# One attention-decode and dense kernel: scores and softmax run two heads ahead of the values, dense and projection weights pass through the value buffers, deeper rings, and the last output-projection rows come last

## The chip, the cores and the metric

The kernel runs on one core of a Trainium2 chip. The metric is the device time in microseconds of one execution. Its engines work side by side, each through its own list of instructions in order: TensorE (PE in the profile; PEld is its weight load), VectorE (DVE), ScalarE (ACT), GpSimd (POOL) and SyncE (SP), which issues the loads. Semaphores tie the lists together.

## What is computed

Two tokens (batch 2, one position each) of width 448 pass through an attention block with a key and value cache and through a dense block with the mish activation; both results are added to the input. The window is the last 4096 of 32768 positions; there are 8 key/value heads of width 256, each shared by 2 query heads.

```python
xn = layernorm(x)                                   # x: 2 x 1 x 448
q = xn @ wq                                         # 16 heads x 256
scores = einsum("bhqd,bhkd->bhqk", q, k[last 4096]) * 256 ** -0.5
o = einsum("bhqk,bhkd->bhqd", softmax(scores), v[last 4096])
attn = o.reshape(2, 1, 4096) @ wo                   # wo: 4096 x 448
h = xn @ w1 + b1                                    # w1: 448 x 1792
dense = (h * tanh(softplus(h))) @ w2                # w2: 1792 x 448
out = x + attn + dense
```

## The kernel before

There are 16 pairs of a key/value head and a batch row, called heads here and numbered i = 0 to 15 (batch row 0, then 1, of each key/value head). Each has a key tile and a value tile of 2 MB (128 partitions, 32 positions each). A head is worked in two halves, so the main loop has 32 steps s; step s is half s % 2 of head s // 2. For one half:

- `turn(s)`: VectorE transposes half of the key tile in blocks (`kt`, L345);
- `scores(s)`: TensorE multiplies the transposed keys with a block-diagonal query `qdiag` (8 matmuls, L357); ScalarE takes the exponential into `p` and its row sums into `rs` (L367);
- `values(s)`: VectorE transposes `p` to `pT` (L380); TensorE multiplies it with half of the value tile (32 matmuls into `o`, L402). In the second half of a head TensorE also sums the denominators (`den`, L389), VectorE takes their reciprocal `rec` and writes the scaled head to `oT` (L415), and for every second head TensorE adds `oT` times the rows `wo` of this key/value head to the result `psA` (8 matmuls, L195, in the helper `add`).

`build_q` has GpSimd fill `qdiag` for a later head. `project` computes the queries from `wq`; `dense_in` and `dense_out` are the dense block, from weights `w1` and `w2` that `load_dense` brings.

All large loads are issued by SyncE in the order of the code: `load_k`, `load_v`, `load_wo`, `load_dense`. Tiles come from pools with a fixed number of buffers: keys 3, values 3, wo 3, with places of their own for `wq`, `w1` and `w2`. A load into a buffer waits until the tile that was there has been used: a key load for the transposition of the second half of the key three heads older (VectorE), a value load for the values three heads older (TensorE). Eight semaphores (DMAHW0 to DMAHW7 in the listings) are used in turn for landings, so a load also waits for the landing of the one eight loads before it. At the end of the code `issue_in_order` pins every engine's instructions to the order in which they are written, so the calls in the loop set each engine's order:

```python
        if s + 1 < NSTEP:
            turn(s + 1)
        if s < NSTEP:
            scores(s)
        if s >= 1:
            values(s - 1)
```

`values(s - 1)` thus stands on TensorE between `scores(s)` and `scores(s + 1)`. Dense loads are issued at step 3, `dense_in` follows step 9 and `dense_out` step 11. After the last step VectorE and ScalarE copy `psA` to `res`, and SyncE stores it.

Of the kernel before, what the change touches and what calls it, by code (L numbers as in the profile page):

```python
# [11 lines left out]
BF16 = mybir.dt.bfloat16  # L12
FP32 = mybir.dt.float32
# [21 lines left out]
def kernel(  # L35
# [13 lines left out]
    nc = tc.nc  # L49
    P = 128  # L50
    Q = 32
# [46 lines left out]


    wq_sb = weights.tile([P, NS, HW], BF16)  # L100
    wq_in = A_wq.rearrange("r (x n) -> (r x) n", x=NX).rearrange("(p s) n -> p s n", s=NS)
    SC = NS // 2 + 1
    nc.sync.dma_start(out=wq_sb[:, 0:SC, :], in_=wq_in[:, 0:SC, :])  # L103
    nc.sync.dma_start(out=wq_sb[:, SC:NS, :], in_=wq_in[:, SC:NS, :])  # L104

# [96 lines left out]
    wq_v = wq_sb[:, :, :].rearrange("p s (h m e) -> p s h e m", h=HH, e=NE)  # L202

    def project():
        qT_ps = ps_m.tile([P, HH, NE, NX * Bsz], FP32, tag="m", name="qT_ps")
        for hh in range(HH):
            for e in range(NE):
                for s in range(NS):
                    nc.tensor.matmul(  # L209
                        qT_ps[:, hh, e, :],  # L210
                        lhsT=wq_v[:, s, hh, e, :],
                        rhs=xs[:, s, :, :].rearrange("p x b -> p (x b)"),
                        start=(s == 0),
                        stop=(s == NS - 1),
                    )
# [28 lines left out]
    w1_sb = weights.tile([P, NS, HF], BF16)  # L244
    w2_sb = weights.tile([P, NX, NF, D], BF16)
    act_bf = consts.tile([P, NF, NX, Bsz], BF16)

    def load_dense():
        nc.sync.dma_start(
            out=w1_sb[:],  # L250
            in_=B_w1.rearrange("r (x n) -> (r x) n", x=NX).rearrange("(p s) n -> p s n", s=NS),
        )
        nc.sync.dma_start(
            out=w2_sb[:], in_=B_w2.rearrange("(x q c) d -> q x c d", x=NX, q=P)
        )

    def dense_in():
        w1_v = w1_sb[:].rearrange("p s (q c) -> p s c q", c=NF)
# [38 lines left out]
    def dense_out():  # L297
        for x in range(NX):
# [12 lines left out]
    LAST = (0, TH, TH + TH // 2, T)  # L311
    k_t, kt_t, v_t, p_t, wo_t = {}, {}, {}, {}, {}
# [10 lines left out]
    def load_v(i):  # L323
        kvh, b = heads[i]
        t = v_pool.tile([P, T, Dh], BF16, tag="v", name="v")
        vin = A_v_cache[b, kvh, s0:Sk, :].rearrange("(p t) d -> p t d", p=P)
        cuts = LAST if i == len(heads) - 1 else (0, T)
        for lo, hi in zip(cuts, cuts[1:]):
            nc.sync.dma_start(out=t[:, lo:hi, :], in_=vin[:, lo:hi, :])
        v_t[i] = t  # L330

    def load_wo(kvh):
        w = wo_pool.tile([P, rep, ND * D], BF16, tag="wo", name="wo")
        r0 = kvh * rep * Dh
        nc.sync.dma_start(
            out=w[:],
            in_=A_wo[r0 : r0 + rep * Dh, :].rearrange("(h p c) d -> p h (c d)", h=rep, p=P),
        )
        wo_t[kvh] = w
# [36 lines left out]
    def values(s):  # L376
        i, half = divmod(s, NH)
        kvh, b = heads[i]
        pT = p_pool.tile([P, TH * Q], BF16, tag="pT", name="pT")
        nc.vector.transpose(out=pT[:], in_=p_t.pop(s)[:])  # L380
        pTv = pT[:].rearrange("p (t c) -> p t c", t=TH)
        if half == 0:
            state["o", i] = ps_o.tile([P, ND, rep], FP32, tag="o", name="o")
        po = state["o", i]
        if half == NH - 1:
            rs = state.pop(("rs", i))
            den = ps_den.tile([P, rep], FP32, tag="den", name="den")
            for n in range(NH):
                nc.tensor.matmul(  # L389
                    den[:],  # L390
                    lhsT=rs[:, n : n + 1].to_broadcast([P, P]),
                    rhs=hsel[:],
                    start=(n == 0),
                    stop=(n == NH - 1),
                )
            rec = small.tile([P, rep], FP32, tag="rec", name="rec")
            nc.vector.reciprocal(out=rec[:], in_=den[:])  # L397
        v = v_t[i] if half < NH - 1 else v_t.pop(i)
        vv = v[:].rearrange("p t (m c) -> p t c m", c=ND)
        for t in range(TH):  # L400
            for c in range(ND):
                nc.tensor.matmul(  # L402
                    po[:, c, :],
                    lhsT=vv[:, half * TH + t, c, :],
                    rhs=pTv[:, t, 0:rep],
                    start=(half == 0 and t == 0 and c == 0),
                    stop=(half == NH - 1 and t == TH - 1),
                    skip_group_check=True,
                )
        if half != NH - 1:  # L410
            return
        if b == 0:
# [5 lines left out]
            in1=rec[:].unsqueeze(1).to_broadcast([P, ND, rep]),  # L418
            op=ALU.mult,
        )  # L420
        if b != Bsz - 1:
            return
        w = wo_t.pop(kvh)
        for n in range(NO):
            for h in range(rep):
# [8 lines left out]

    KA = 2
    for i in range(KA):
        load_k(i)
    load_wo(0)
# [4 lines left out]
    for s in range(NSTEP + 1):  # L443
        i, half = divmod(s, NH)
        if half == 0 and i < len(heads):
            if i + KA < len(heads):
                load_k(i + KA)
            load_v(i)
        if s == 3:
            load_dense()  # L450
        if s % (NH * Bsz) == 0 and s // (NH * Bsz) + 1 < Hkv:
            load_wo(s // (NH * Bsz) + 1)
        if s % NH == 0 and 0 < s < NSTEP - NH:
            build_q(s // NH + 1)
        if s + 1 < NSTEP:
            turn(s + 1)
        if s < NSTEP:
            scores(s)
        if s >= 1:
            values(s - 1)  # L460
        if s == 9:
            dense_in()
        if s == 11:
            dense_out()

# [35 lines left out]
```

## Time and profile before

| | |
|---|---|
| median of three runs | 202.58 us (202.35 to 204.18) |
| the profiled execution | 204.15 us, of which the span is 202.4 us |
| read from HBM | 77.67 MB |
| busy: TensorE, VectorE, ScalarE, GpSimd | 139.2, 102.9, 25.5, 24.9 us |
| granted TensorE clock, mean | 0.79 of full |

The span is the time from the first to the last instruction that the profile shows; the rest of the execution lies around it. Idle time of an engine costs nothing unless something on the way to the end waits for it, so the rows to look at are those of the resource that is always busy, and what happens when it isn't. "PEclk" and the column ahead of the DMA share in the windows view are the clock that TensorE was granted, as a part of full speed.

### The profile page before, as it was taken

How to read it: one execution, taken by the hardware profiler on the slowest of the kernel's cores; microseconds unless marked ns; L12 is line 12 of the kernel's file. 1: busy time of each engine (PE TensorE's matmuls, PEld its weight loads, DVE VectorE, ACT ScalarE, POOL GpSimd, SP SyncE). 2: the span in 40 equal slices, each digit the busy share in tenths (PEclk: the TensorE clock that was granted, in tenths of full speed). 3: DMA queues.
4: the chain of work that ended last, by engine and by line, in shares of the span. 5: the costliest groups of instructions: out<-in, count | busy, mean ns of one | idle time of the engine just before them, and what ended most of it. 6: DMA issues, size and time to landing. Idle time of an engine off the chain costs nothing.

```text
span 202.4 us, 3790 instructions
## 1 busy us (share of the span) xinstructions
PE 139.2 (69%) x1624; PEld 82.0 (41%) x1624; DVE 102.9 (51%) x137; ACT 25.5 (13%) x69; POOL 24.9 (12%) x138
## 2 busy tenths in 40 slices
PE   0262802969906849799999388856976596849993
PEld 0051202526303425565766145533534353426472
DVE  4607660191910564137748917473656455562921
ACT  5000200111010201101112102020112011201120
POOL 7006210020020100200202201120022002000000
PEclk9999995575555878855899969697979797975797
DMA  6999999999999999997999999999999999999200
GB/s 224 425 437 421 434 421 415 431 417 430 422 410 437 427 426 419 423 424 243 434 427 421 431 434 405 429 424 427 407 442 427 418 419 430 424 421 406 83 0 2
DMA packets 7802, 77.90 MB, mean 385 GB/s; under 512 B 741, under 2 KB 2793, under 8 KB 3306
## 3 DMA queue, kind: packets, MB, share of 16 engines
q1 hardware_dynamic: 7780, 77.66, 91.9%
q8 instruction: 12, 0.20, 0.4%
q14 instruction: 4, 0.03, 0.0%
q10 hardware_dynamic: 6, 0.01, 0.0%
HBM read 77.67 MB, written 0.00 MB: 384 GB/s over the span
## 4 chain that ended last, share of the span: by engine, by line
DMA 61%; PE 20%; DVE 15%; SPq 1%; issue 1%; ACT 1%
DMA v<-in_A_v_cache_dram 53%; DVE kt L345 12%; PE sc L357 10%; DMA k<-in_A_k_cache_dram 8%; PE o L402 6%; DVE pT L380 2%; PE hT_ps L263 2%; PE psA L195 1%; PE den L389 1%; SPq L318 1%; PE hT_ps L272 1%; DVE oT L415 0%; ACT p L367 0%; SPq L104 0%; SPq L103 0%
## 5 line engine op out<-in xcount | busy, mean ns | idle before, releaser
L357 PE MATMUL sc<-kt,qdiag 128*128 128x512 bf16 x256 | 86.3, 496 | 3.5 <-DVE kt L345 3.5
L345 DVE STREAM_TRANSPOSE kt<-k 128x2048 f32<-128x2048 f32 x32 | 73.1, 2287 | 2.3 <-DMA k<-in_A_k_cache_dram 2.3
L402 PE MATMUL o<-pT,v 128*128 128x2 bf16 x1024 | 30.8, 164 | 43.9 <-DMA v<-in_A_v_cache_dram 43.2
L402 PEld LDWEIGHTS <-v 128*128 128x128 bf16 x1024 | 30.8, 101 | 52.1 <-DMA v<-in_A_v_cache_dram 49.8
L357 PEld LDWEIGHTS <-qdiag 128*128 128x128 bf16 x256 | 27.4, 116 | 44.6 <-issue 29.4
L367 ACT ACTIVATE p<-sc 128x512 bf16<-128x512 f32 x32 | 19.1, 597 | 163.3 <-PE sc L357 163.3
L238 POOL COPY qdiag<-qrep 32x8 bf16<-32x8 bf16 x128 | 21.0, 187 | 143.2 <-PE sc L357 128.0
L397 DVE RECIPROCAL rec<-den 128x2 f32<-128x2 f32 x16 | 2.6, 166 | 62.5 <-PE den L389 62.5
L380 DVE STREAM_TRANSPOSE pT<-p 128x512 bf16<-128x512 bf16 x32 | 21.6, 674 | 3.0 <-ACT p L367 3.0
L389 PEld LDWEIGHTS den<-hsel,rs 128*128 128x128 f32 x64 | 12.9, 250 | 4.6 <-issue 3.3
L195 PE MATMUL psA<-wo,oT 128*2 128x224 bf16 x64 | 8.9, 291 | 2.0 <-DVE oT L415 2.0
L389 PE MATMUL den<-hsel,rs 128*128 128x2 f32 x64 | 10.2, 264 | 0.0
L415 DVE TENSOR_TENSOR oT<-o,rec 128x4 bf16<-128x4 f32 x16 | 2.6, 165 | 11.0 <-PE o L402 11.0
L209 PE MATMUL qT_ps<-xs,wq_sb 128*128 128x4 bf16 x112 | 3.3, 166 | 5.8 <-DMA wq_sb<-in_A_wq_dram 3.2
L195 PEld LDWEIGHTS <-oT 128*2 128x2 bf16 x64 | 5.2, 91 | 3.9 <-DVE oT L415 2.7
L367 ACT ACTIVATION_READ_ACCUMULATOR p<-sc 128x1 f32 x32 | 6.2, 194 | 0.0
L209 PEld LDWEIGHTS <-wq_sb 128*128 128x128 bf16 x112 | 3.1, 104 | 6.3 <-DMA wq_sb<-in_A_wq_dram 6.3
L163 PE MATMUL xnT_ps<-ident,xn_bf 2*128 2x2 bf16 x7 | 0.5, 166 | 5.0 <-DVE xn_bf L127 5.0
L282 DVE COPY h_sb<-hT_ps 128x28 f32<-128x28 f32 x1 | 0.2, 188 | 7.0 <-PE hT_ps L272 7.0
L263 PE MATMUL hT_ps<-xs,w_sb 128*128 128x4 bf16 x49 | 3.7, 195 | 0.0
L218 DVE CAST qT<-qT_ps 128x64 bf16<-128x64 f32 x1 | 0.2, 225 | 6.7 <-PE qT_ps L209 6.7
L263 PEld LDWEIGHTS <-w_sb 128*128 128x128 bf16 x49 | 3.2, 150 | 0.1
(40 smaller groups left out, 24.9 us busy)
## 6 DMA issues: line engine op xcount, KB each, us to landing
k<-in_A_k_cache_dram SPq DMA_DIRECT2D x16, 2048.0 KB, 16.1
v<-in_A_v_cache_dram SPq DMA_DIRECT2D x15, 2048.0 KB, 20.6
wo<-in_A_wo_dram SPq DMA_DIRECT2D x8, 448.0 KB, 21.1
w_sb<-in_B_w_dram SPq DMA_DIRECT2D x2, 1568.0 KB, 28.0
wq_sb<-in_A_wq_dram SPq DMA_DIRECT2D x1, 2048.0 KB, 7.6
wq_sb<-in_A_wq_dram SPq DMA_DIRECT2D x1, 1536.0 KB, 10.8
v<-in_A_v_cache_dram SPq DMA_DIRECT2D x1, 1024.0 KB, 13.0
v<-in_A_v_cache_dram SPq DMA_DIRECT2D x2, 512.0 KB, 14.3
```

Source lines behind the costliest of these rows:

```text
L195: nc.tensor.matmul(psA[n][:, :], lhsT=lhsT, rhs=rhs, skip_group_check=True, **flags)
L209: nc.tensor.matmul(qT_ps[:, hh, e, :], lhsT=wq_v[:, s, hh, e, :], rhs=xs[:, s, :, :].rearrange("p x b -> p (x b)"), start=(s == 0), stop=( ...
L238: nc.gpsimd.tensor_copy(out=tv[rows, :, e, j * Q : j * Q + rep], in_=qrep[rows, :, h0 : h0 + rep, e, x, b],)
L263: nc.tensor.matmul(hT_ps[:, c, :, :].rearrange("p x b -> p (x b)"), lhsT=w1_v[:, s, c, :], rhs=xs[:, s, :, :].rearrange("p x b -> p (x b)" ...
L345: nc.vector.transpose(out=kt[:].bitcast(FP32), in_=k[:, half * TH * Dh : (half + 1) * TH * Dh].bitcast(FP32),)
L357: nc.tensor.matmul(psc[:], lhsT=qdiag[i % NW][:, n * NE + e, :], rhs=ktv[:, n, e, :, :], start=(n == 0 and e == 0), stop=(n == NB - 1 and ...
L367: nc.scalar.activation(out=p_sb[:], in_=psc[:].rearrange("p t c -> p (t c)"), func=ACT.Exp, scale=scale, accum_out=state["rs", i][:, s % N ...
L380: nc.vector.transpose(out=pT[:], in_=p_t.pop(s)[:])
L389: nc.tensor.matmul(den[:], lhsT=rs[:, n : n + 1].to_broadcast([P, P]), rhs=hsel[:], start=(n == 0), stop=(n == NH - 1),)
L397: nc.vector.reciprocal(out=rec[:], in_=den[:])
L402: nc.tensor.matmul(po[:, c, :], lhsT=vv[:, half * TH + t, c, :], rhs=pTv[:, t, 0:rep], start=(half == 0 and t == 0 and c == 0), stop=(half ...
L415: nc.vector.tensor_tensor(out=oT[:, :, :, b], in0=po[:], in1=rec[:].unsqueeze(1).to_broadcast([P, ND, rep]), op=ALU.mult,)
```

## The change

Four things are changed.

1. `values` is split. `turn_p(s)` holds the transposition of `p`, the denominators and their reciprocal; `values(i)` holds all 64 value matmuls of a head and `oT`; `mix(kvh)` holds the wo matmuls. The loop goes over heads, and `values` of head i - 2 stands behind both sets of scores of head i. `pT` gets seven buffers, `p` three.
2. The pool `weights` is gone: the two parts of `wq`, then `w1` and `w2` are tiles of the value pool, which has five buffers; values 1 to 4 go into the buffers that they leave. The key pool has four buffers.
3. The dense loads are issued behind the first key, `dense_in` follows the scores of head 0, `dense_out` those of head 1.
4. `load_wo` of a key/value head stands behind its second value load in place of one key/value head ahead. The last value load is cut in halves (before: a half and two quarters), the last wo load in two pieces that are issued last of all.

```diff
-    weights = ctx.enter_context(tc.tile_pool(name="weights", bufs=1))
-    k_pool = ctx.enter_context(tc.tile_pool(name="kk", bufs=3))
-    v_pool = ctx.enter_context(tc.tile_pool(name="vv", bufs=3))
+    k_pool = ctx.enter_context(tc.tile_pool(name="kk", bufs=4))
+    v_pool = ctx.enter_context(tc.tile_pool(name="vv", bufs=5))
...
-    p_pool = ctx.enter_context(tc.tile_pool(name="pp", bufs=2))
+    p_pool = ctx.enter_context(tc.tile_pool(name="pp", bufs=3))
...
+    def v_tile(n):
+        t = v_pool.tile([P, T * Dh], BF16, tag="v", name="v")
+        return t[:, 0:n]
...
+    def turn_p(s):
+        pT = p_pool.tile([P, TH * Q], BF16, tag="pT", name="pT", bufs=7)
+        nc.vector.transpose(out=pT[:], in_=p_t.pop(s)[:])
+        pT_t[s] = pT
         i, half = divmod(s, NH)
+        if half != NH - 1:
+            return
+        rs = state.pop(("rs", i))
+        den = ps_den.tile([P, rep], FP32, tag="den", name="den")
...
+        nc.vector.reciprocal(out=state["rec", i][:], in_=den[:])
...
+    def mix(kvh):
+        oT = state["oT"]
         w = wo_t.pop(kvh)
-        for n in range(NO):
-            for h in range(rep):
+        for h in range(rep):
+            for n in range(NO):
                 for c in range(ND):
...
+    load_k(0)
+    load_dense()
+    load_k(1)
     project()
     build_q(0)
     build_q(1)
     turn(0)
...
+    for i in range(NK + KA):
+        if i + 2 < NK:
+            load_k(i + 2)
+        if i < NK:
+            load_v(i, parts=1 if i < NK - 1 else 2)
+            kvh, b = heads[i]
+            if b == Bsz - 1:
+                load_wo(kvh, parts=1 if i < NK - 1 else 2)
+            for half in range(NH):
+                s = i * NH + half
+                if s + 1 < NSTEP:
+                    turn(s + 1)
+                scores(s)
+                if s >= 1:
+                    turn_p(s - 1)
+            if i + 2 < NK:
+                build_q(i + 2)
+        if i == NK:
+            turn_p(NSTEP - 1)
+        if i == 0:
             dense_in()
-        if s == 11:
+        if i == 1:
             dense_out()
+        if i >= KA:
+            values(i - KA)
+            kvh, b = heads[i - KA]
+            if b == Bsz - 1:
+                mix(kvh)
```

Three places in the engines' order show the move. A row has the line, the operation, what it writes and from what, the tile's shape, and in brackets the engines or landing semaphores for which it waits.

SyncE at the start, before: from the two halves of `wq` on.

```order
L103 DMA wq_sb<-in_A_wq_dram 128x8192
L104 DMA wq_sb<-in_A_wq_dram 128x6144
L318 DMA k<-in_A_k_cache_dram 128x8192 x2
L335 DMA wo<-in_A_wo_dram 128x2x896
L318 DMA k<-in_A_k_cache_dram 128x8192
L329 DMA v<-in_A_v_cache_dram 128x8192 [waits DMAHW0_49]
L335 DMA wo<-in_A_wo_dram 128x2x896 [waits DMAHW1_49]
L318 DMA k<-in_A_k_cache_dram 128x8192 [waits DMAHW4_49,DMAHW2_49,DVE_49]
L329 DMA v<-in_A_v_cache_dram 128x8192 [waits DMAHW3_49]
L249 DMA w_sb<-in_B_w_dram 128x6272
L253 DMA w_sb<-in_B_w_dram 128x2x3136 [waits DMAHW5_49]
```

SyncE at the start, with the change; tiles named v that come from `wq` or `w` (the dense weights) are buffers of the value pool.

```order
L109 DMA v<-in_A_wq_dram 128x8192
L109 DMA v<-in_A_wq_dram 128x6144
L325 DMA k<-in_A_k_cache_dram 128x8192
L255 DMA v<-in_B_w_dram 128x6272
L260 DMA v<-in_B_w_dram 128x2x3136
L325 DMA k<-in_A_k_cache_dram 128x8192
L325 DMA k<-in_A_k_cache_dram 128x8192 [waits DMAHW0_49]
L336 DMA v<-in_A_v_cache_dram 128x8192 [waits DMAHW1_49]
L325 DMA k<-in_A_k_cache_dram 128x8192 [waits DMAHW2_49]
L336 DMA v<-in_A_v_cache_dram 128x8192 [waits DMAHW3_49,PE_49]
L345 DMA wo<-in_A_wo_dram 128x2x896 [waits DMAHW4_49]
L325 DMA k<-in_A_k_cache_dram 128x8192 [waits DMAHW5_49,DVE_49]
```

The dense weights moved from behind the second value to behind the first key, the wo load from behind the second key to behind the second value, and the fourth key no longer waits for VectorE.

VectorE in one head of the steady state, before: from the transposition of a head's first key half (which waits for the key's landing) to the scaled head `oT`.

```order
L345 STREAM_TRANSPOSE kt<-k 128x2048 [waits DMAHW7_49]
L380 STREAM_TRANSPOSE pT<-p 128x512 [waits Activation_49]
L345 STREAM_TRANSPOSE kt<-k 128x2048
L380 STREAM_TRANSPOSE pT<-p 128x512 [waits Activation_49]
L397 RECIPROCAL rec<-den 128x2 [waits PE_49]
L415 TENSOR_TENSOR oT<-o,rec 128x4 [waits DVE_49,PE_49]
L345 STREAM_TRANSPOSE kt<-k 128x2048 [waits DMAHW2_49]
```

VectorE in the same stretch with the change.

```order
L352 STREAM_TRANSPOSE kt<-k 128x2048 [waits DMAHW6_49,DVE_49]
L385 STREAM_TRANSPOSE pT<-p 128x512 [waits Activation_49]
L422 TENSOR_TENSOR oT<-o,rec 128x4 [waits DVE_49,PE_49]
L352 STREAM_TRANSPOSE kt<-k 128x2048 [waits DVE_49]
L385 STREAM_TRANSPOSE pT<-p 128x512 [waits Activation_49]
L401 RECIPROCAL rec<-den 128x2 [waits PE_49]
L352 STREAM_TRANSPOSE kt<-k 128x2048 [waits DMAHW0_49,DVE_49]
```

Before, `rec` and `oT` stand together and belong to the head whose scores are just done; with the change `rec` stands in front of the next key's transposition, and `oT`, which waits for TensorE's values, belongs to a head two back.

SyncE at the end, before: from the last key load on.

```order
L318 DMA k<-in_A_k_cache_dram 128x8192 [waits DMAHW2_49,DVE_49]
L329 DMA v<-in_A_v_cache_dram 128x8192 [waits DMAHW3_49,PE_49]
L329 DMA v<-in_A_v_cache_dram 128x8192 [waits DMAHW6_49,DMAHW4_49,PE_49]
L329 DMA v<-in_A_v_cache_dram 128x4096 [waits DMAHW5_49,DMAHW0_49,PE_49]
L329 DMA v<-in_A_v_cache_dram 128x2048
L329 DMA v<-in_A_v_cache_dram 128x2048 [waits DMAHW7_49]
```

SyncE at the end with the change.

```order
L325 DMA k<-in_A_k_cache_dram 128x8192 [waits DMAHW0_49,DVE_49]
L336 DMA v<-in_A_v_cache_dram 128x8192 [waits DMAHW1_49,PE_49]
L345 DMA wo<-in_A_wo_dram 128x2x896 [waits DMAHW2_49]
L336 DMA v<-in_A_v_cache_dram 128x8192 [waits DMAHW3_49,PE_49]
L336 DMA v<-in_A_v_cache_dram 128x4096 [waits DMAHW4_49,PE_49]
L336 DMA v<-in_A_v_cache_dram 128x4096 [waits DMAHW5_49]
L345 DMA wo<-in_A_wo_dram 128x896 [waits DMAHW6_49]
L345 DMA wo<-in_A_wo_dram 128x896 [waits DMAHW7_49]
```

The last wo load stood ahead of this stretch, in front of the last key, and is now in two pieces behind the last value; the wo load seen in the middle is that of the head pair before.

More of the change, by code (lines that the diff above doesn't have):

```diff
@@ L297, in dense_out @@
     def dense_out():
+        w2_sb = dense.pop("w2")
         for x in range(NX):
@@ L374, in scores, with values @@
         p_t[s] = p_sb
-    def values(s):
+    def turn_p(s):
+        pT = p_pool.tile([P, TH * Q], BF16, tag="pT", name="pT", bufs=7)
+        nc.vector.transpose(out=pT[:], in_=p_t.pop(s)[:])
+        pT_t[s] = pT
         i, half = divmod(s, NH)
-        kvh, b = heads[i]
[L379 to L400, printed above, removed]
+        if half != NH - 1:
+            return
+        rs = state.pop(("rs", i))
+        den = ps_den.tile([P, rep], FP32, tag="den", name="den")
+        for n in range(NH):
+            nc.tensor.matmul(
+                den[:],
+                lhsT=rs[:, n : n + 1].to_broadcast([P, P]),
+                rhs=hsel[:],
+                start=(n == 0),
+                stop=(n == NH - 1),
+            )
+        state["rec", i] = small.tile([P, rep], FP32, tag="rec", name="rec", bufs=4)
+        nc.vector.reciprocal(out=state["rec", i][:], in_=den[:])
+    def values(i):
+        kvh, b = heads[i]
+        po = ps_o.tile([P, ND, rep], FP32, tag="o", name="o")
+        vv = v_t.pop(i).rearrange("p t (m c) -> p t c m", c=ND)
+        for t in range(T):
+            half, th = divmod(t, TH)
+            pTv = pT_t[i * NH + half][:].rearrange("p (t c) -> p t c", t=TH)
             for c in range(ND):
@@ L403, in values @@
                     po[:, c, :],
[L404 to L407, printed above, removed]
+                    lhsT=vv[:, t, c, :],
+                    rhs=pTv[:, th, 0:rep],
+                    start=(t == 0 and c == 0),
+                    stop=(t == T - 1),
                     skip_group_check=True,
                 )
-        if half != NH - 1:
-            return
         if b == 0:
@@ L433, in values @@
                     )
+    NK = len(heads)
     KA = 2
-    for i in range(KA):
-        load_k(i)
-    load_wo(0)
+    load_k(0)
+    load_dense()
+    load_k(1)
     project()
```

71 lines of the change are left out of this document (26 added, 45 removed).

## The prediction

> **What bounds the kernel now.** I read the page's head, the forty slices and the DMA queue first, since they say whether one resource is full all the time.
>
> ```profile
> span 202.4 us, 3790 instructions
> PE 139.2 (69%) x1624; PEld 82.0 (41%) x1624; DVE 102.9 (51%) x137; ACT 25.5 (13%) x69; POOL 24.9 (12%) x138
> DMA  6999999999999999997999999999999999999200
> GB/s 224 425 437 421 434 421 415 431 417 430 422 410 437 427 426 419 423 424 243 434 427 421 431 434 405 429 424 427 407 442 427 418 419 430 424 421 406 83 0 2
> q1 hardware_dynamic: 7780, 77.66, 91.9%
> ```
>
> The DMA row is at 9 from the second slice to the 37th, with one 7; every compute engine has slack. So the 77.66 MB set the time, and two things lie outside that stream: the hole in slice 18, counted from 0 (243 GB/s), and the last three slices, in which almost nothing is loaded while the kernel still runs. The windows view gives their sizes (columns from the right: GB/s, DMA share, granted TensorE clock).
>
> ```profile
> 4.00:90.00 86.00, 52.02 (x592) 30.33 (x593) 36.92 (x62) 7.96 (x22) 10.88 (x65) 0.75 1.01 424
> 20.00:35.00 15.00, 5.49 (x48) 2.51 (x47) 7.09 (x5) 1.38 (x4) 2.02 (x13) 0.82 1.01 421
> 85.00:90.00 5.00, 5.00 (x56) 3.98 (x55) 0.88 (x4) 0.23 (x1) 0.00 (x0) 0.50 1.00 426
> 90.00:95.00 5.00, 4.58 (x45) 2.73 (x44) 3.90 (x7) 0.69 (x2) 0.00 (x0) 0.50 0.80 262
> 93.00:93.50 0.50, 0.19 (x8) 0.19 (x8) 0.31 (x2) 0.03 (x1) 0.00 (x0) 0.50 0.08 33
> 95.00:100.00 5.00, 5.00 (x56) 3.10 (x55) 5.00 (x4) 0.69 (x2) 1.33 (x8) 0.73 0.95 406
> 100.00:185.00 85.00, 63.59 (x730) 36.70 (x728) 47.54 (x49) 11.45 (x33) 9.28 (x56) 0.85 1.01 424
> 185.00:190.00 5.00, 4.75 (x47) 2.56 (x48) 4.11 (x5) 0.26 (x2) 0.00 (x0) 0.51 0.63 255
> 190.00:195.00 5.00, 5.00 (x84) 3.39 (x83) 2.64 (x5) 1.38 (x4) 0.00 (x0) 1.00 0.01 3
> ```
>
> The stream runs at 424 GB/s before and after the hole. A 2.097 MB key or value load is thus 4.95 us of stream, a wo load (0.459 MB) 1.08 us, a head (one key, one value, half a wo) 10.4 us. The hole costs 5 x (424 - 262)/424 = 1.9 us and then 5 x (424 - 406)/424 = 0.2 us: 2.1 us. Who made it stands in SyncE's waits and its timeline:
>
> ```profile
> SPq L318 <- DVE kt L345: 120.2, 13, 18.4
> 22.28 0.43 SPq L249 DMA_DIRECT2D w_sb<-in_B_w_dram  x1
> 73.80 0.38 SPq L329 DMA_DIRECT2D v<-in_A_v_cache_dram  x1
> 92.69 0.33 SPq L318 DMA_DIRECT2D k<-in_A_k_cache_dram  x1
> 88.76 0.19 DVE L282 COPY h_sb<-hT_ps 128x28 f32<-128x28 f32 x1 [7.00 <-PE hT_ps L272]
> 90.36 2.31 DVE L345 STREAM_TRANSPOSE kt<-k 128x2048 f32<-128x2048 f32 x1
> ```
>
> Columns of a timeline row: start, length, engine. Between 74.2 and 92.69 nothing was issued: the key load waits for VectorE to transpose the second half of an older key, and VectorE stood at the dense part, behind TensorE, behind a value load. What was queued ran out at about 92.
>
> The tail, last value landing to the end (landing is counted from issue, 175.25, in the row as 175.3):
>
> ```profile
> L329 SPq DMA_DIRECT2D v<-in_A_v_cache_dram x2: 416/421/426, 174.8 to 175.3; - x2
> DMA to landing us min/median/max: 13.9/14.3/14.6
> PE o L402 <- DMA v<-in_A_v_cache_dram: 43.2, 12, 9.5
> 180.09 1.01 PE L402 MATMUL o<-pT,v 128*128 128x2 bf16 x32 [3.94 <-DMA v<-in_A_v_cache_dram]
> 186.28 1.65 PE L195 MATMUL psA<-wo,oT 128*2 128x224 bf16 x8 [0.26 <-DVE oT L415]
> 197.72 0.94 PE L402 MATMUL o<-pT,v 128*128 128x2 bf16 x32 [0.29 <-DVE rec L397]
> 198.91 0.93 PE L195 MATMUL psA<-wo,oT 128*2 128x224 bf16 x8 [0.26 <-DVE oT L415]
> 199.88 0.34 ACT L468 CAST res<-psA 2x224 bf16<-2x224 f32 x1 [2.96 <-PE psA L195]
> ```
>
> The last value piece landed at 175.25 + 14.6 = 189.85. TensorE used it only at 197.72: it had stood 43.2 us in all for values, with transposed keys ready behind that wait, and had four sets of scores and six half heads of values left at 180.09. So 202.37 - 189.85 = 12.5 us of tail, most of it a backlog.
>
> **The change part by part.** Counts of instructions are equal on TensorE and VectorE, so no work is taken away; the gain has to come from those two places.
>
> 1. *The hole.* By the order, the dense loads stand right behind the first key, and the dense matmuls run in head 0. No wait of VectorE can then hold the queue as long. The rows for the start and for VectorE's turn in a head:
>
> ```profile
> 16.90 4.50 DVE L345 STREAM_TRANSPOSE kt<-k 128x2048 f32<-128x2048 f32 x2 [0.68 <-DMA k<-in_A_k_cache_dram]
> 23.03 2.31 DVE L345 STREAM_TRANSPOSE kt<-k 128x2048 f32<-128x2048 f32 x1 [1.63 <-DMA k<-in_A_k_cache_dram]
> L380 DVE STREAM_TRANSPOSE pT<-p 128x512 bf16<-128x512 bf16 x32 | 21.6, 674 | 3.0 <-ACT p L367 3.0
> L415 DVE TENSOR_TENSOR oT<-o,rec 128x4 bf16<-128x4 f32 x16 | 2.6, 165 | 11.0 <-PE o L402 11.0
> 12.03 3.04 PE L209 MATMUL qT_ps<-xs,wq_sb 128*128 128x4 bf16 x108 [3.23 <-DMA wq_sb<-in_A_wq_dram]
> ```
>
> Steady state: key j+4 leaves when key j is transposed, some 5.5 us after it landed (2.31, then 0.67 for pT, 0.17 for oT, 2.31 for the second half), or when the load eight before it has landed. Behind key j stand value j-2, key j+1 and so on to value j+1; at that moment six key and value loads and a wo are still queued, some 13 MB or 30 us. A value load waits for values five heads older, which lie further back still.
>
> Start, in landings: key 0 still lands at 16.9; the 3.2 MB of dense weights push key 1 from 23.0 to about 30.6. Value 1, the first load into a buffer that held wq, waits for the projection (done at 15.1) with 32 us queued; key 4 for key 0's transposition (21.4); key 5 for key 1's second half at about 37, with six loads (26 us) queued. The late start of TensorE costs nothing as long as a head takes it less than the stream's 10.4 us. So the hole goes. What the *last* engine of the sixteen regains is not shown: at least the half microsecond at 33 GB/s in which nearly all stood, at most 2.1 us. I take 1.8, near the mean's 2.1, since the slowest engine drains the queue longest and idles least. Last landing: 189.85 - 1.8 = 188.05.
>
> 2. *The tail.* Scores run two heads ahead, so behind the last landings stand only values and wo. The last value half lands 1.08 us of wo before the end, at 186.97. From there the old rows hold: the values matmuls started at 197.72 and the span ended at 202.37, 4.65 us. 186.97 + 0.05 + 4.65 = 191.7. The half clock takes the wo matmuls from 0.93 to 1.65 and adds 0.7: 192.4. By the wo path: 188.05 + 0.05 + half of 1.65 + 2.53 (the old 199.84 to 202.37) = 191.5, hidden behind the value path. I take 192.4, since TensorE waits between these landings, and behind such waits the before kernel was at half clock (1.65 at 186.28, clock 0.51).
>
> 3. *At nothing:* deeper rings, seven pT buffers, the pieces of the last loads (46 loads on both sides), the reciprocal moved into `turn_p`. The transfers hide them; uncovered, the largest is one 0.4 us issue.
>
> Sum: 202.4 - 192.4 = 10.0 us. The profiled execution took 204.15 (span and 1.75 around it), 1.6 above the median, so its own time would become 194.15, and the median 202.58 - 10.0 = **192.6**.
>
> **A rule weighed here: the clock.**
>
> ```profile
> 84.05 0.51 PE L263 MATMUL hT_ps<-xs,w_sb 128*128 128x4 bf16 x7
> 88.65 3.59 PE L357 MATMUL sc<-kt,qdiag 128*128 128x512 bf16 x8
> 92.04 0.85 PE L389 MATMUL den<-hsel,rs 128*128 128x2 f32 x4
> 93.31 0.99 PE L402 MATMUL o<-pT,v 128*128 128x2 bf16 x32 [0.42 <-DVE rec L397]
> 98.45 2.84 PE L195 MATMUL psA<-w_sb,act_bf 128*2 128x224 bf16 x28
> 128.04 3.21 PE L357 MATMUL sc<-kt,qdiag 128*128 128x512 bf16 x8
> 132.56 1.90 PE L357 MATMUL sc<-kt,qdiag 128*128 128x512 bf16 x8
> ```
>
> A set of scores is 3.59 us at half clock and 1.90 at full. TensorE was busy 9.6 of the 10 us from 85 to 95, and the granted clock was 0.50 in both windows and 0.73 in the next. The Trainium skill ("TensorE: Matmul & The Clock Gate", section "What's actually happening") says that some 3.4 us of sustained work release the clock, and that an idle window of that length takes it away. By that rule two sets of scores back to back end warm, rival B falls away, and the last wo matmuls, behind waits, run cold: 192.4 as above. By the rows the first half does not hold here: half clock lasted through 10 us of small and large matmuls, so B stays.
>
> **Rivals.**
> A (forecast), 0.68: 192.6.
>
> B, 0.15: TensorE still has a backlog at the end, at half clock. Behind key 15 come 7.21 MB, 17.0 us, so it lands at 171.0. Transposed 173.3; scores 176.9; denominators 177.7; scores 181.3; values 13 183.3; oT and wo 185.4; den 186.2; values 14 and 15 190.2; oT and wo 192.2; end 194.8 (scores 3.59, denominators 0.85, a head's values 1.98, oT with its waits 0.43, wo 1.65, end 2.53). That is 7.6 less than before: 195.0. For it: 3.59 in several rows. Against: with little between them the second set ran in 1.90 after a first of 3.21; one warm set and its followers save 2.7 us, and the landings decide again.
>
> C, 0.06: the change does not keep the queue full: a hole of 2.1 us opens elsewhere, at a wait for the load eight before. 194.7. Against: the 26 us queued at the tightest wait found.
>
> D, 0.04: the small last pieces drain slower. The last two old pieces of 0.52 MB landed at 188.7 and 189.85, 1.15 us apart where the stream's rate gives 1.24, which speaks against it. If the two wo pieces of 0.23 MB took three times the stream's 1.08 us, the last would land at 190.2 and the wo path end at 193.6, 1.2 above A: 193.8. The Trainium skill ("DMA: Bandwidth & Descriptors", sections "Rules for kernel authors" and "Bandwidth") asks for at least 1 MiB per load, and gives 341 GB/s for one such load and 138 for one of 64 KB. An estimate by that page is 1.3 to 3.3 us for the two pieces, an end between 191.7 and 193.7; the rows with 0.52 MB pieces show no such loss.
>
> E, 0.04, no change: TensorE at half clock all the way. A head is 2 x 3.59 + 0.85 + 2 x 0.99 + 0.83 = 10.8 us against 10.4 of stream; from 19.3, sixteen heads (173) and the dense part (7.5) end at 200.1, and with 3.1 of end it is 203.2. Against: 0.75 and 0.85 granted over long windows.
>
> F, 0.03, slower: the rate of the stream falls because seven loads are queued at all times in place of about four. Its point is where 77.66 MB take 12 us more than 183: below 398 GB/s the kernel is over 1% slower; at 395 it takes about 205.5. Against: 421 in 20 to 35, when the dense weights (issued at 22.28) and others were put behind others still queued, and 424 over the long windows.
>
> **How the numbers follow.** The range: downward a whole hole regained (0.3), full clock at the end (0.7) and the last engines' drain of about a microsecond shortened: 190.5. Upward to B and C, 195.2. That leaves out E, F and parts of A and B, under 2 in 10. Within 1% (about what a measurement of this kernel tells from no change) is E, 0.04; slower is F, 0.03; the rest, 0.93, is faster.
>
> **What would show it.** Right: the GB/s row at 405 to 440 without a gap from slice 1 on; the key waits on SyncE short of starving it; last landing near 188; the last wo matmuls some 4 us behind it and no scores after 182. Wrong: a slice below 300 in the middle (C), scores or values 14 after the last landing (B), TensorE busy throughout at clock 0.5 (E), every slice below 400 (F).

## The result, and the profile after

The changed kernel takes 194.68 us (median of 4, 194.53 to 194.9) against 202.93 us for the kernel before: ratio 0.9586, 95% interval 0.9538 to 0.9635, 8.2 us less. (The three executions of the section on the time before are among the four of this 202.93.) Here and below, medians are over all executions, while ratios leave out the slow ones, those more than 1.5% above the fastest of the same kernel. The profiled execution took 194.53 us, its span is 192.7 us (before: 204.15 and 202.4).

The page of the changed kernel, head and forty slices:

```profile
span 192.7 us, 3810 instructions
PE 130.4 (68%) x1624; PEld 81.3 (42%) x1624; DVE 102.2 (53%) x137; ACT 25.5 (13%) x69; POOL 24.8 (13%) x138
PEclk9999996699995799669975998599957979589965
DMA  6999999999999999999999999999999999999960
GB/s 211 424 447 408 427 427 435 428 435 402 431 422 428 425 415 428 435 418 414 429 425 432 420 416 430 428 425 411 428 432 428 403 434 422 432 414 429 410 253 2
DMA 96%; PE 1%; SPq 1%; issue 0%; ACT 0%; DVE 0%
```

The 7 in the DMA row is gone, and so are the empty slices at the end but one. The chain that ended last is now 96% transfers; before it was 61%, with 20% TensorE and 15% VectorE. The work is the same: TensorE has 1624 matmuls in both and is busy for 130 in place of 139 us, at a mean granted clock of 0.845 in place of 0.792.

SyncE's waits in the changed kernel (columns: us in total, times, longest):

```profile
SPq L345 <- DMA v<-in_A_v_cache_dram: 30.3, 7, 5.8
SPq L336 <- DMA k<-in_A_k_cache_dram: 27.2, 6, 4.7
SPq L325 <- DMA k<-in_A_k_cache_dram: 27.0, 6, 4.6
SPq L325 <- DVE kt L352: 6.7, 1, 6.7
```

Before, a key load waited up to 18.4 us for VectorE. Now SyncE waits for VectorE once, for 6.7 us, and otherwise mostly for the landing of the load eight before, 4 to 6 us at a time, with the seven loads between them still queued. The page says the same: a key load takes 32.5 us from issue to landing (median) in place of 16.1. The end of the changed kernel on TensorE, then rows of the windows view (last three columns: granted clock, DMA share, GB/s), one microsecond each:

```profile
180.32 0.93 PE L201 MATMUL psA<-wo,oT 128*2 128x224 bf16 x8 [0.26 <-DVE oT L422]
182.29 1.75 PE L411 MATMUL o<-pT,v 128*128 128x2 bf16 x64 [0.50 <-DMA v<-in_A_v_cache_dram]
184.78 1.01 PE L411 MATMUL o<-pT,v 128*128 128x2 bf16 x32 [0.73 <-DMA v<-in_A_v_cache_dram]
187.26 1.01 PE L411 MATMUL o<-pT,v 128*128 128x2 bf16 x32 [1.47 <-DMA v<-in_A_v_cache_dram]
188.53 1.65 PE L201 MATMUL psA<-wo,oT 128*2 128x224 bf16 x8 [0.26 <-DVE oT L422]
```

```profile
183.00:184.00 1.00, 1.00 (x42) 0.96 (x39) 0.00 (x0) 0.00 (x0) 0.00 (x0) 1.00 0.97 401
184.00:185.00 1.00, 0.27 (x10) 0.23 (x9) 0.17 (x1) 0.00 (x0) 0.00 (x0) 0.55 0.94 379
185.00:186.00 1.00, 0.79 (x30) 0.70 (x27) 0.00 (x0) 0.00 (x0) 0.00 (x0) 0.50 0.75 283
186.00:187.00 1.00, 0.00 (x0) 0.00 (x0) 0.00 (x0) 0.00 (x0) 0.00 (x0) 0.50 0.30 114
187.00:188.00 1.00, 0.74 (x28) 0.75 (x29) 0.00 (x0) 0.00 (x0) 0.00 (x0) 0.50 0.20 68
```

TensorE has no scores left after 178.5; it waits for each of the last landings and works them off in a microsecond. The stream thins out from 184 on. A DMA share of 0.30 in 186 to 187 is what about five busy engines of the sixteen would give, so most seem to be done while a few are not, and the last landings hang on those; these views do not show single transfer engines.

### The profile page after: what moved, and what is told of

Read it like the earlier page. It is cut to its first block, busy times and chain, and to the rows that moved or that the text cites. A ratio compares the mean times of both kernels' runs of the same rounds, so it can differ in the third digit from the quotient of the medians.

```text
span 192.7 us, 3810 instructions
## 1 busy us (share of the span) xinstructions
PE 130.4 (68%) x1624; PEld 81.3 (42%) x1624; DVE 102.2 (53%) x137; ACT 25.5 (13%) x69; POOL 24.8 (13%) x138
## 3 DMA queue, kind: packets, MB, share of 16 engines
q1 hardware_dynamic: 7652, 77.66, 96.1%
## 4 chain that ended last, share of the span: by engine, by line
DMA 96%; PE 1%; SPq 1%; issue 0%; ACT 0%; DVE 0%
DMA v<-in_A_v_cache_dram 51%; DMA k<-in_A_k_cache_dram 18%; DMA wo<-in_A_wo_dram 17%; DMA v<-in_B_w_dram 10%; PE psA L201 1%; PE o L411 1%; SPq L109 0%; SPq L325 0%; ACT res L484 0%; DVE oT L422 0%; SPq L336 0%
## 5 line engine op out<-in xcount | busy, mean ns | idle before, releaser
L364 PE MATMUL sc<-kt,qdiag 128*128 128x512 bf16 x256 | 75.0, 443 | 14.4 <-DVE kt L352 14.3
L364 PEld LDWEIGHTS <-qdiag 128*128 128x128 bf16 x256 | 26.1, 111 | 50.5 <-issue 24.1
L201 PE MATMUL psA<-wo,oT 128*2 128x224 bf16 x64 | 12.5, 370 | 31.3 <-DVE oT L422 31.3
L411 PEld LDWEIGHTS <-v 128*128 128x128 bf16 x1024 | 27.9, 97 | 6.3 <-DMA v<-in_A_v_cache_dram 3.0
L411 PE MATMUL o<-pT,v 128*128 128x2 bf16 x1024 | 28.1, 163 | 2.7 <-DMA v<-in_A_v_cache_dram 2.7
L201 PEld LDWEIGHTS <-oT 128*2 128x2 bf16 x64 | 6.5, 111 | 34.6 <-DVE oT L422 32.0
L393 PEld LDWEIGHTS den<-hsel,rs 128*128 128x128 f32 x64 | 11.7, 227 | 3.8 <-issue 2.1
L215 PE MATMUL qT_ps<-xs,v 128*128 128x4 bf16 x112 | 3.3, 166 | 6.1 <-DMA v<-in_A_wq_dram 6.1
L215 PEld LDWEIGHTS <-v 128*128 128x128 bf16 x112 | 3.1, 104 | 6.6 <-DMA v<-in_A_wq_dram 6.6
L270 PE MATMUL hT_ps<-xs,v 128*128 128x4 bf16 x49 | 3.7, 195 | 0.0
L270 PEld LDWEIGHTS <-v 128*128 128x128 bf16 x49 | 3.2, 149 | 0.3
L201 PE MATMUL psA<-v,act_bf 128*2 128x224 bf16 x28 | 2.8, 259 | 0.0
## 6 DMA issues: line engine op xcount, KB each, us to landing
k<-in_A_k_cache_dram SPq DMA_DIRECT2D x16, 2048.0 KB, 32.5
```

The source lines that it names most:

```text
L201: nc.tensor.matmul(psA[n][:, :], lhsT=lhsT, rhs=rhs, skip_group_check=True, **flags)
L215: nc.tensor.matmul(qT_ps[:, hh, e, :], lhsT=wq_v[s][:, hh, e, :], rhs=xs[:, s, :, :].rearrange("p x b -> p (x b)"), start=(s == 0), stop=( ...
L270: nc.tensor.matmul(hT_ps[:, c, :, :].rearrange("p x b -> p (x b)"), lhsT=w1_v[:, s, c, :], rhs=xs[:, s, :, :].rearrange("p x b -> p (x b)" ...
L364: nc.tensor.matmul(psc[:], lhsT=qdiag[i % NW][:, n * NE + e, :], rhs=ktv[:, n, e, :, :], start=(n == 0 and e == 0), stop=(n == NB - 1 and ...
L393: nc.tensor.matmul(den[:], lhsT=rs[:, n : n + 1].to_broadcast([P, P]), rhs=hsel[:], start=(n == 0), stop=(n == NH - 1),)
L411: nc.tensor.matmul(po[:, c, :], lhsT=vv[:, t, c, :], rhs=pTv[:, th, 0:rep], start=(t == 0 and c == 0), stop=(t == T - 1), skip_group_check ...
```

## The experiments

They ran in three sets, each on one chip beside the kernel before, whose medians were 203.24, 203.34 and 203.37 us; ratios are against it, with 95% intervals.

**The kernel before once more.** No edit.

> The kernel before once more, unchanged, for a second profile: its executions differ by more than the changed kernel's (202.35 to 204.18 against 194.53 to 194.9). Theory: the hole differs from one execution to the next, and with it the place where TensorE falls behind; the time outside the span is 1.8 us again. Rival: the hole is the same and the tail differs.

201.95 us, span 200.2. SyncE and the windows of the second profile:

```profile
92.75 0.33 SPq L318 DMA_DIRECT2D k<-in_A_k_cache_dram  x1
```

```profile
90.00:95.00 5.00, 3.85 (x46) 2.36 (x45) 3.96 (x8) 0.69 (x2) 0.00 (x0) 0.84 0.75 256
185.00:190.00 5.00, 4.70 (x60) 2.72 (x57) 4.80 (x4) 0.69 (x2) 0.00 (x0) 1.00 0.65 261
```

```profile
179.99 1.00 PE L402 MATMUL o<-pT,v 128*128 128x2 bf16 x32 [3.76 <-DMA v<-in_A_v_cache_dram]
185.42 0.93 PE L195 MATMUL psA<-wo,oT 128*2 128x224 bf16 x8 [0.26 <-DVE oT L415]
186.28 1.91 PE L357 MATMUL sc<-kt,qdiag 128*128 128x512 bf16 x8
```

The rival is right: the hole is nearly the same (92.75 and 256 GB/s; 92.69 and 262 before), value 13 is used at the same moment (179.99; 180.09 before), and from there this execution needs 20.2 us and the first one 22.3. In 185 to 190 it was granted the full clock, the first one 0.51. In both, the clock fell to half at about 180, when TensorE had waited for value 13; in this one it was full again from 184 on, in the first one from 190 on, with the same instructions in the same order. So these two executions differ by the clock that the backlog is granted, and the profile that I predicted from was a long one. That the whole spread of the kernel before comes from this is likely, but two profiles don't show it.

**Dense loads early, alone.**

```diff
-    for i in range(KA):
-        load_k(i)
+    load_k(0)
+    load_dense()
+    load_k(1)
     load_wo(0)
...
-        if s == 9:
+        if s == 1:
             dense_in()
-        if s == 11:
+        if s == 3:
             dense_out()
```

> The kernel before with one part of the change alone: the dense loads behind the first key, dense_in after step 1 and dense_out after step 3; values still stand between the two sets of scores, rings as before. Theory: the hole at 92 goes, the backlog at the end stays; the span falls by 1.5 to 2.1 us and the tail behind the last value landing stays near 12 us. Rival 1: the hole only moves to another place where a key load waits for VectorE (span as before, a slice under 300 GB/s elsewhere). Rival 2: the dense part was the cause of the backlog too (tail under 8 us, gain over 5 us).

205.29 us, ratio 1.0088 (1.0038 to 1.0139): slower than before by some 0.9%. The profiled execution took 203.71. TensorE and the windows:

```profile
41.78 1.02 PE L402 MATMUL o<-pT,v 128*128 128x2 bf16 x32 [15.97 <-DMA v<-in_A_v_cache_dram]
```

```profile
50.00:55.00 5.00, 4.58 (x45) 2.79 (x43) 3.98 (x5) 0.69 (x2) 0.00 (x0) 0.50 0.59 193
```

Rival 1: the hole moves, from 92 to 51, and is larger (5 x (425 - 193)/425 = 2.7 us). Behind the dense weights value 0 comes at 41.8 in place of 34.0, and with values between the scores everything stands 16 us for it. SyncE was held by VectorE for up to 20.5 us. So moving the dense part doesn't remove the hole. In its new place it again stands between TensorE's wait for a value and VectorE's next transposition (dense matmuls from 42.6 to 47.2, transposition at 48.97, key load at 51.30).

**The run-ahead alone.** The kernel before with `turn_p`, `values(i)` and `mix` as in the change, values one head behind, `pT` in five buffers to hold what waits, and nothing else.

```diff
         if s >= 1:
-            values(s - 1)
+            turn_p(s - 1)
+        r = i - 1 if half == 1 else (i - 1 if s == NSTEP else -1)
+        if r >= 0:
+            values(r)
+            if heads[r][1] == Bsz - 1:
+                mix(heads[r][0])
```

> The kernel before with one part of the change alone: values, as one block of a head, run one head behind the scores. Rings of three keys and three values, load order, weights' own buffers, the dense part's place and the last pieces stay as before. Theory: the run-ahead by itself takes VectorE and TensorE off the wait for values; a key is then held only until value i-1 has landed, with four loads (20 us) queued, so no hole, and the tail is short: span 193.4 to 194.5, time 195.3 to 196.5. Rival: the old rings run dry without the new order of loads and a hole of 2 us or more stays: 197.5 to 199.

197.45 us (197.42 to 197.7), ratio 0.9735 (0.967 to 0.9801); no hole:

```profile
GB/s 218 421 439 426 419 429 414 429 423 408 449 426 418 423 429 426 410 429 426 426 403 436 423 431 423 419 419 429 429 410 429 429 423 413 430 426 426 392 71 2
```

```profile
178.87 1.87 PE L404 MATMUL o<-pT,v 128*128 128x2 bf16 x64 [3.65 <-DMA v<-in_A_v_cache_dram]
182.57 2.61 PE L357 MATMUL sc<-kt,qdiag 128*128 128x512 bf16 x8
191.16 1.65 PE L195 MATMUL psA<-wo,oT 128*2 128x224 bf16 x8 [0.26 <-DVE oT L415]
```

So the run-ahead by itself closes the hole, with the old rings and the dense part in its old place, and brings 5.8 of the 8.2 us. Other than I had expected, it doesn't take VectorE off TensorE's wait; the waits and the key load that made the hole before are:

```profile
SPq L318 <- DVE kt L345: 96.5, 13, 17.1
85.68 0.33 SPq L318 DMA_DIRECT2D k<-in_A_k_cache_dram  x1
```

A key load is still held for up to 17.1 us (18.4 before), but this one leaves at 85.68 in place of 92.69, before the queue has run empty. The time is a microsecond above the expected 195.3 to 196.5, at the edge of the rival's range, though without the rival's hole: after value 13 (178.87) a head of scores is still to do, and value 13 lands late, because both last wo loads lie ahead of it.

**Values between the scores again, in the changed kernel.** Deep rings, load order and last pieces as changed; a helper `step(s)` does `turn_p(s)`, the half head of values and, every fourth time, `mix`.

```diff
                 if s >= 1:
-                    turn_p(s - 1)
+                    step(s - 1)
...
-        if i >= KA:
-            values(i - KA)
-            kvh, b = heads[i - KA]
-            if b == Bsz - 1:
-                mix(kvh)
```

> The changed kernel with its rings, its load order and its last pieces, but values stand again in halves between the sets of scores, as before the change. Theory: no hole, but the backlog comes back: from the landing of value 13 (about 176) TensorE needs the 22.3 us that it took before (180.04 to 202.37), so the span is 198 to 198.5 and the time 199.5 to 200.5. Rival: rings and load order bring the gain, the run-ahead is not needed; 194.7 as the changed kernel.

198.95 us (196.91 to 199.39), ratio 0.9773 (0.9701 to 0.9845), span 196.7 in the profiled execution. No slice is under 300 until the end, though SyncE is held by VectorE for up to 19.3 us, as before (18.4). TensorE, from value 13 on:

```profile
176.36 0.95 PE L415 MATMUL o<-pT,v 128*128 128x2 bf16 x32 [2.63 <-DMA v<-in_A_v_cache_dram]
177.18 3.40 PE L364 MATMUL sc<-kt,qdiag 128*128 128x512 bf16 x8
193.27 0.93 PE L201 MATMUL psA<-wo,oT 128*2 128x224 bf16 x8 [0.26 <-DVE oT L428]
```

The backlog is back: from 176.36 it takes 20.3 us, as long as in the second profile of the kernel before, the one with the better clock; I had expected the 22.3 of the first one, and so a time of 199.5 or more. There is no hole without the run-ahead; what covers it, the depth of the rings or the new order of loads, is for the next run. So the hole can be closed without the run-ahead, but the tail cannot be shortened without it.

**The same with shallow rings.** As the last one, with three key and four value buffers.

```diff
-    k_pool = ctx.enter_context(tc.tile_pool(name="kk", bufs=4))
-    v_pool = ctx.enter_context(tc.tile_pool(name="vv", bufs=5))
+    k_pool = ctx.enter_context(tc.tile_pool(name="kk", bufs=3))
+    v_pool = ctx.enter_context(tc.tile_pool(name="vv", bufs=4))
```

> The changed kernel's load order and last pieces, but values between the scores as before, with three key and four value buffers. Beside the run with the same order and deep rings (198.95, no slice under 300, SyncE held by VectorE for up to 19.3 us) it tells what the rings do without the run-ahead. Theory: without the run-ahead only depth covers those 19 us; with three key buffers the hole is back (a slice under 300) and the time is 200.5 to 203. Rival: depth does not matter here either: 198.5 to 199.5.

201.55 us (198.65 to 203.47), ratio 0.9875 (0.9813 to 0.9937). The profiled execution (203.4 us) shows the hole in slices 9 and 10:

```profile
GB/s 241 415 440 410 432 439 429 423 426 303 343 432 419 423 426 429 419 432 416 432 416 436 413 429 423 432 400 440 426 423 414 438 423 426 414 430 402 139 0 2
```

303 and 343 in place of "under 300", but the hole is there and the time in the range: in this execution the rings had to cover VectorE's wait, and three key and four value buffers did not. The evidence is one profile, and of one of the longest of ten executions. The shortest (198.65) took no longer than the deep rings' median (198.95), and the intervals of the two ratios overlap by a little (0.9813 against 0.9845), so what the depth is worth in time is not settled.

**Shallow rings with the run-ahead.** The same edit on the changed kernel.

> The changed kernel with three key buffers and four value buffers in place of four and five; all else as changed. Theory: the holes come from VectorE being held behind TensorE's wait for values, not from the depth of the rings; with the run-ahead a key is transposed some 5.5 us after its landing, when five loads (24 us) are still queued, so the stream stays without a hole: 194.4 to 195.4. Rival: the deeper rings keep the stream full, and with the old key ring a slice under 300 GB/s comes back: 196.5 to 198.5.

195.21 us (195.12 to 195.55), ratio 0.9614 (0.9563 to 0.9664). No slice under 400 until the end; SyncE's longest wait for VectorE is 6.7 us:

```profile
SPq L325 <- DVE kt L352: 68.0, 13, 6.7
```

The theory holds: with the run-ahead of two heads the stream has no hole even with shallow rings. The time is 0.5 us above the changed kernel in another set, and the intervals of the ratios overlap.

**One head of run-ahead in place of two.**

```diff
-    KA = 2
+    LAG = 1
...
-        if i >= KA:
-            values(i - KA)
+        if LAG <= i < NK + LAG:
+            values(i - LAG)
```

> The changed kernel with values one head behind the scores in place of two. Theory: key 15 lands some 17 us ahead of the last wo piece, its two sets of scores need 2.3 + 2.3 + 5.5 to 7.2 us, and value 14 lands 11 us behind key 15, so one head of run-ahead hides all but about half a microsecond: 194.5 to 195.5. Rival: two heads are needed, TensorE carries a backlog of a head's scores (3.8 to 7 us) into the end: 198 to 201.

194.88 us (194.71 to 195.33), ratio 0.9595 (0.9545 to 0.9646): the same as two. Its end hangs on TensorE:

```profile
176.42 1.84 PE L411 MATMUL o<-pT,v 128*128 128x2 bf16 x64 [3.68 <-DMA v<-in_A_v_cache_dram]
187.68 1.74 PE L411 MATMUL o<-pT,v 128*128 128x2 bf16 x64
189.67 1.01 PE L201 MATMUL psA<-wo,oT 128*2 128x224 bf16 x8 [0.26 <-DVE oT L422]
```

The last values run without a wait, so it is at the edge: the second head of run-ahead buys slack, not time. Value 13 is used 2.45 us sooner than in the run-ahead alone. The two last wo loads, 0.92 MB or 2.2 us of stream, lie behind value 13 here and ahead of it there: that would account for most of the 2.6 us between these two runs, that is, of what the rest of the change brings.

**wo not last.**

```diff
-            if b == Bsz - 1:
-                load_wo(kvh, parts=1 if i < NK - 1 else 2)
+            if b == 0:
+                load_wo(kvh)
```

> The changed kernel with every wo load behind the first value of its pair of heads and in one piece, so that the last value half is the last load. Theory: the end hangs on the value path, and the last value half lands 1.08 us of stream later (188.3 in place of 187.2), so the time rises by 1.0 us to 195.7. Rival: the last wo pieces drain slowly, being small, and set the end themselves; then the time falls or stays (193.5 to 194.7).

196.55 us (195.93 to 196.95), ratio 0.9671 (0.9619 to 0.9724): 1.9 us more than the changed kernel, where 1.0 was expected. The last value half is used at 188.64, 1.4 us later than at 187.26, and the span is 194.0, 1.3 longer.

```profile
188.64 1.01 PE L411 MATMUL o<-pT,v 128*128 128x2 bf16 x32 [0.85 <-DMA v<-in_A_v_cache_dram]
```

The mechanism is as expected. The other half microsecond lies outside the span: 2.95 us in this execution, 1.7 to 2.8 in the other three, against 1.8 to 2.1 in the other profiled executions. What it is stays open.

**Smaller last pieces.**

```diff
+    CUTS = (0, TH, TH + TH // 2, TH + 3 * TH // 4, T)
...
-        for u in range(parts):
-            ts = slice(u * T // parts, (u + 1) * T // parts)
+        cuts = (0, T) if parts == 1 else CUTS
+        for lo, hi in zip(cuts, cuts[1:]):
+            ts = slice(lo, hi)
```

> The changed kernel with the last value load in pieces of 16, 8, 4 and 4 of its 32 positions. Theory: the end hangs on the value matmuls behind the last landing; 8 of them (0.25 us) stand there in place of 32 (1.01 us), so the time falls by 0.75 us to 193.9. Rival: small pieces drain more slowly, or the last wo piece (landed at 188.3) becomes the bound: 194.5 to 195.5.

194.32 us (194.06 to 194.45), ratio 0.9564 (0.9519 to 0.9609): some 0.4 below the changed kernel, measured in another set and with overlapping intervals, in place of 0.75.

```profile
187.57 0.37 PE L414 MATMUL o<-pT,v 128*128 128x2 bf16 x8 [0.28 <-DMA v<-in_A_v_cache_dram]
188.20 1.65 PE L201 MATMUL psA<-wo,oT 128*2 128x224 bf16 x8 [0.26 <-DVE oT L425]
```

The last values take 0.37 in place of 1.01, but the last piece is used 0.3 later (187.57), so half of the gain is lost.

**Keeping the clock up.** The first version adds four matmuls ahead of head 15's values and six between their halves; the second (with the smaller pieces) four ahead of head 14's and three ahead of each half of head 15's.

```diff
+    def warm(n):
+        w = ps_sc.tile([P, TH, Q], FP32, tag="sc", name="sc")
+        src = pT_t[NSTEP - 2][:].rearrange("p (t c) -> p t c", t=TH)
+        for _ in range(n):
+            nc.tensor.matmul(w[:], lhsT=ident[:], rhs=src, start=True, stop=True)
...
+            if i == NK - 1 and th == 0:
+                warm(4 if half == 0 else 6)
```

> The changed kernel with ten added matmuls of 128x512 whose result is not used: four ahead of the last head's values and six between their halves, in time in which TensorE waits for landings. Theory: the last wo matmuls ran at half clock (1.65 us) because TensorE waited; with the clock kept up they take 0.93 and the time falls by 0.7 to 194.0. Rival: the clock does not come up, the added matmuls take 0.43 us each and push the last values back: 195 to 197.

195.45 us, ratio 0.9621 (0.9579 to 0.9664), 0.8 above the changed kernel of another set: the rival's time.

```profile
186.66 2.72 PE L407 MATMUL sc<-pT,ident 128*128 128x512 bf16 x6
189.17 1.01 PE L419 MATMUL o<-pT,v 128*128 128x2 bf16 x32
190.44 0.93 PE L201 MATMUL psA<-wo,oT 128*2 128x224 bf16 x8 [0.26 <-DVE oT L430]
```

The six took 0.45 us each at half clock and held the last values back to 189.17. Other than the rival says, the clock then did come up: wo in 0.93.

> The changed kernel with the last value load in pieces of 16, 8, 4 and 4 and with ten added matmuls of 128x512 whose result is not used: four ahead of the values of head 14, while the clock is still full, and three ahead of each half of head 15's. Theory: spread so, they keep the clock up from 180 on and fit into the waits (0.22 us each), the last wo matmuls take 0.93 in place of 1.65, and the time falls by 0.7 below the pieces alone: 193.6. Rival: the clock drops all the same, each takes 0.43, and the last values start later: 194.5 to 195.5.

194.46 us (193.76 to 194.88), ratio 0.9589 (0.9532 to 0.9646); 0.3 below the changed kernel in the same set, with ranges that overlap. In the profiled execution, the fastest of the six with 193.76, they did what they should:

```profile
PEclk9999995799995899579965968597858879589997
```

```profile
187.63 0.35 PE L424 MATMUL o<-pT,v 128*128 128x2 bf16 x8 [0.29 <-DMA v<-in_A_v_cache_dram]
188.24 1.07 PE L201 MATMUL psA<-wo,oT 128*2 128x224 bf16 x8 [0.26 <-DVE oT L435]
```

The last four digits are 9, 9, 9 and 7, where the changed kernel has 9, 9, 6 and 5, and wo takes 1.07 in place of 1.65. The other five executions took 194.22 to 194.88, against 194.06 to 194.45 for the smaller pieces alone, so a gain of time is not shown.

**The changed kernel once more.** No edit.

> The changed kernel once more, unchanged, beside the others of this set on one chip. Theory: 194.7 as before, with a spread below half a microsecond, since its end hangs on the loads and not on the clock that TensorE is granted. Rival: it varies as much as the kernel before (2 us or more).

194.76 us (194.68 to 194.97), ratio 0.9601 (0.9551 to 0.9652). In the same set the kernel before ran from 201.74 to 205.35. The spread of 0.3 against 3.6 us fits an end that hangs on loads, but doesn't show it by itself: the run-ahead alone, whose end is a backlog of TensorE, stayed within 0.3 us too, over four executions.

## Why the prediction was right, and which term was off

The time came out at 194.68, inside 190.5 to 195.2 and 2.1 above the 192.6. That the range held is in part luck: its upper end was set by rivals B and C, which did not come, and not by the term that was off.

- *The hole goes.* Right: no slice under 400 from slice 1 to 37. Its reason was half wrong. I gave the early dense part as one cause; alone it moved the hole and cost a little. The run-ahead alone closes it: VectorE still stands behind TensorE's values, but the key load leaves 7 us sooner. In the changed kernel, with two heads of run-ahead, the longest hold is 6.7 us, even with shallow rings. Without the run-ahead it closes too, by deeper rings as far as one profile each of the two runs with values between the scores shows.
- *What the last transfer engine regains.* I took 1.8 us and a last landing at 188.05. The last wo piece was issued at 166.4 and landed 21.9 us later, at 188.3: 1.55.

```profile
L345 SPq DMA_DIRECT2D wo<-in_A_wo_dram x1: 328/328/328, 166.4 to 166.4; - x1
DMA to landing us min/median/max: 21.9/21.9/21.9
```

- *The tail.* Right to a few tenths: last value half used at 187.26 (187.02 predicted), half clock for wo (1.65; why is taken up below), span 192.7 (192.4). Own time 194.53, against 194.15 worked out for the profiled execution.
- *From the profiled execution to the median: the term that was off.* I took the 10.0 us off the median of before, 202.58. That execution was 1.6 us above this median, and I carried the difference over. The second profile of before puts it in the tail that the change removes: it has nearly the same hole and a tail 2.1 us shorter, at a better clock. So the sum's own end, 194.15, was the better forecast of the median, and the gain from median to median is 8.2, not 10.0. This step is 1.55 of the 2.1 us; the last landing (0.25) and a few tenths behind it are the rest.
- *Rival B* did not come: from the second head on, a set of scores behind a wait took 3.1 to 3.6, the sets after it 1.9, and the landings decided. With one head of run-ahead it is nearly there, at no cost in time. *C*: no new hole; the waits for the load eight before are there, with 30 us queued. *D*: the two wo pieces landed within 1.1 us of the value half. *E* and *F*: 0.85 granted in the mean of 4 to 180, and 424 GB/s in that window with seven loads queued, the same rate as with about four before. (F's 205.5 is a slip: 395 GB/s makes the 77.66 MB 13.4 us longer, which gives 206.0.)

```profile
4.00:180.00 176.00, 123.41 (x1476) 75.81 (x1476) 98.95 (x127) 22.76 (x66) 21.42 (x129) 0.85 1.01 424
```

- *The rule on the clock* ("TensorE: Matmul & The Clock Gate" in the Trainium skill, section "What's actually happening"). Its half on waiting agrees with the kernel before: TensorE stood from 176.15 to 180.09, and the granted clock fell from 1.00 to 0.50 within 179 to 180. It doesn't explain the 1.65 at the end, which I put down to waits: the longest wait there is 1.47 us, and the clock fell at the start of 184 to 185 (0.55), right behind 1.75 us of two-column matmuls that had kept TensorE busy for all of 183 to 184. Its half on sustained work held for the scores, which ran in 1.9 behind a first set, although I had set it aside. What counts as work stays open: ten added 512-column matmuls in those waits kept the clock at full until 190 in the profiled execution, but whether by their width or by filling the waits was not separated. So the half clock at the end was forecast right for a reason that the runs do not show.

## What to carry to other kernels

Where transfers bound a kernel, put every step that needs only early data ahead of the step that waits for late data, on each engine's own list: here one head of run-ahead on TensorE was worth 5.8 us, and without it the deeper rings and the new order of loads closed the hole in the middle of the run but left the backlog at its end. Then order the loads by what is left to do behind them, the ones with the least work last. And work a forecast out to the end of the new chain rather than taking a difference off a median: the part of an execution that varies may be the part that the change removes.

## What the runs showed of the hardware that was not expected

The sixteen transfer engines do not seem to end together. The rate fell from 401 GB/s in 183 to 184 to 283, 114 and 68 in the windows from 185 on, with a DMA share of 0.75, 0.30 and 0.20, while the last load had been queued since 166.4; so some engines ended some 3 us ahead of the slowest. Which ones, and why, was not tried, nor whether the last loads can be shared out better. Pieces of 0.26 MB, queued behind others, cost no more than 0.3 us at the end.
